# A recurrent-memory attention layer and its gradients: 32-row slots in four head groups, with the first eight rows of every segment batched outside the chains

## The chip, the cores and the metric

The kernel runs on one core of one Trainium2 chip. The metric is the device time of one execution in microseconds (us). A time below is the median of several executions, with the lowest and highest where they matter. A ratio is the mean time of one kernel's fast runs over the mean of the fast runs of the kernel before in the same rounds on the same chip, so it is not quite the ratio of the medians quoted beside it.

Names of the engines in the profile: PE is TensorE (matmul), PEld its weight load, DVE is VectorE, ACT is ScalarE, POOL is GpSimd, SP is SyncE; SPq, ACTq and POOLq are the queues from which these engines issue DMAs.

## The reference, cut to what matters

The reference computes a layer and all its gradients. The expensive half is attention with a recurrent memory: the sequence of 2,048 rows is cut into 64 segments of 32; in front of each stand 8 memory rows, which are the outputs of the 8 memory rows of the segment before.

```python
# B,S,Dm = 1,2048,512 ; H,Dh = 32,128 ; M,seg = 8,32 ; bf16
xn = layernorm(x); mem = mem0
mask = (idx[:,None] < M) | (idx[:,None] >= idx[None,:])      # memory rows see all 40
for s in range(64):
    h = concat([mem, xn[:, 32*s:32*s+32]])                    # 40 rows
    q, k, v = h@Wq, h@Wk, h@Wv                                # per head
    p = softmax(where(mask, q@k.T * Dh**-0.5, -1e9))
    o = einsum('hte,hed->td', p@v, Wo)
    mem = o[:8]; outs.append(o[8:])
out = x + concat(outs) + mlp(xn)         # mlp: relu(xn@w1+b1)**2 @ w2 + b2, F = 1792
# returned: out and the gradients of x, mem0, Wq, Wk, Wv, Wo, w1, b1, w2, b2
```

Forward and backward are therefore two chains of 64 dependent segments. One fact is used by the change: every row of a segment sees the memory rows, a segment row sees only earlier segment rows, and only the output of the 8 memory rows is carried on.

## The kernel before

Everything is laid out with the 40 rows of a segment on 40 of the 128 partitions. Projections go two at a time, one on rows 0 to 39 and one on rows 64 to 103 of the result; softmax works on 40 partitions x 12 heads; P is turned on PE, head by head.

```python
def proj2(dst, col0, nch):                 # two 512-column chunks at a time
    for fj in range(0, nch, 2):
        for dc in range(DC):
            nc.tensor.matmul(psA[:], lhsT=hT[:, dc, :], rhs=Wqkv[:, dc, ...], tile_position=(0, 0))
            nc.tensor.matmul(psB[64:64 + L, :], lhsT=hT[:, dc, :], rhs=Wqkv[:, dc, ...], tile_position=(0, 64))
        nc.any.tensor_copy(dst[...], psA[:]); nc.any.tensor_copy(dst[...], psB[64:64 + L, :])
# ... softmax on [40, 12 heads, 40] pieces, three pieces a segment ...
for i in range(nh):                        # P and gS are turned on PE, 40x40 at a time
    transpose_to(ps[:, i * L:(i + 1) * L], Pb[:, hh, :])
# ... the backward chain stores its gradients transposed, 960 KB a segment:
dma(S_GQKVT[s], gqkvT_s[:])
# ... and a stage after the chains loads them (segt), sums the input gradient in PSUM (ps_gxnA),
#     turns them and stores them in natural order (S_GN); then the weight gradients load S_GN.
```

Of the kernel before, what the change touches and what calls it, by code (L numbers as in the profile page):

```python
# [12 lines left out]
P = 128  # L13
# [13 lines left out]
def kernel(  # L27
# [71 lines left out]
    psp = ctx.enter_context(tc.tile_pool(name="psp", bufs=8, space=bass.MemoryType.PSUM))  # L99
    dram = ctx.enter_context(tc.tile_pool(name="dram", bufs=1, space=bass.MemoryType.DRAM))  # L100

    def pst(shape, dt=F32, name="ps"):
        return psp.tile(shape, dt, name=name, tag="ps")

    S_HN = dram.tile([NROWS, D], BF16, name="S_HN")
# [6 lines left out]
    S_ON = dram.tile([NROWS, HD], BF16, name="S_ON")  # L112
    S_GMEM = dram.tile([NSEG * M, D], BF16, name="S_GMEM")
    S_QKN = dram.tile([NSEG, L, 2 * HD], BF16, name="S_QKN")
    S_VT = dram.tile([NSEG, P, H, L], BF16, name="S_VT")
    S_P = dram.tile([NSEG, L, H, L], BF16, name="S_P")
    S_GQKVT = dram.tile([NSEG, P, 3, H, L], BF16, name="S_GQKVT")
    S_GN = dram.tile([NROWS, 3 * HD], BF16, name="S_GN")
# [8 lines left out]
    maskb = const.tile([L, L], F32, name="maskb")  # L127
    nc.gpsimd.memset(maskb[:], 0.0)
    nc.gpsimd.affine_select(
        maskb[:], maskb[:], pattern=[[-1, L]], compare_op=ALU.is_ge, fill=-1e9, base=0, channel_multiplier=1  # L130
    )
    nc.gpsimd.memset(maskb[0:M, :], 0.0)
    maskrep = const.tile([L, GMAX, L], F32, name="maskrep")
    for j in range(GMAX):
        nc.vector.tensor_copy(maskrep[:, j, :], maskb[:])
    ones_col = const.tile([P, 1], BF16, name="ones_col")
    nc.vector.memset(ones_col[:], 1.0)
    zeros_bf = const.tile([P, D], BF16, name="zeros_bf")
    nc.vector.memset(zeros_bf[:], 0.0)
    NCG = 4  # L140
    assert H % NCG == 0 and (3 * H) % NCG == 0 and M <= 32
    sel8 = const.tile([P, M], F32, name="sel8")
    nc.gpsimd.memset(sel8[:], 0.0)
    for g in range(NCG):
        nc.gpsimd.affine_select(
            sel8[:], sel8[:], pattern=[[-1, M]], compare_op=ALU.not_equal, fill=1.0, base=-32 * g, channel_multiplier=1
        )
# [7 lines left out]
    with tc.tile_pool(name="p0", bufs=1) as p0:  # L155
        xnN = p0.tile([P, TC, D], BF16, name="xnN")
        with tc.tile_pool(name="p0a", bufs=1) as p0a:
            xN = p0a.tile([P, TC, D], BF16, name="xN")
            dma(xN[:], xflat.rearrange("(c p) d -> p c d", p=P))
            ssum = p0a.tile([P, TC], F32, name="ssum")  # L160
            nc.vector.tensor_reduce(ssum[:], xN[:], axis=AX.X, op=ALU.add)
            nc.scalar.mul(mean_t[:], ssum[:], 1.0 / D)
            xc = p0a.tile([P, TC, D], BF16, name="xc")
            nc.vector.tensor_tensor(
                out=xc[:], in0=xN[:], in1=mean_t[:].unsqueeze(2).to_broadcast([P, TC, D]), op=ALU.subtract
            )
            sq = p0a.tile([P, TC, D], BF16, name="sq")
            nc.vector.tensor_tensor(out=sq[:], in0=xc[:], in1=xc[:], op=ALU.mult)
            var_t = p0a.tile([P, TC], F32, name="var_t")
            nc.vector.tensor_reduce(var_t[:], sq[:], axis=AX.X, op=ALU.add)  # L170
            veps = p0a.tile([P, TC], F32, name="veps")
            nc.vector.tensor_scalar(
                out=veps[:], in0=var_t[:], scalar1=1.0 / D, scalar2=EPS, op0=ALU.mult, op1=ALU.add
            )
            sdev = p0a.tile([P, TC], F32, name="sdev")
            nc.scalar.sqrt(sdev[:], veps[:])
            nc.vector.reciprocal(rstd_t[:], sdev[:])
            nc.vector.tensor_tensor(
                out=xnN[:], in0=xc[:], in1=rstd_t[:].unsqueeze(2).to_broadcast([P, TC, D]), op=ALU.mult
            )  # L180
        dma(S_HN[0:S, :].rearrange("(c p) d -> p c d", p=P), xnN[:])
        xnT = p0.tile([P, DC, S], BF16, name="xnT")
        gN = p0.tile([P, TC, D], BF16, name="gN")
        dma(gN[:], gflat.rearrange("(c p) d -> p c d", p=P))
        gT = p0.tile([P, DC, S], BF16, name="gT")
        npb = 1024 // P
        for src, dstT in ((xnN, xnT), (gN, gT)):
            for dc in range(DC):
                c0 = 0
                while c0 < TC:  # L190
                    n = min(npb, TC - c0)
                    ps = pst([P, n * P], BF16, name="ps_tr")
                    for j in range(n):
                        transpose_to(ps[:, j * P:(j + 1) * P], src[:, c0 + j, dc * P:(dc + 1) * P])
                    nc.any.tensor_copy(dstT[:, dc, c0 * P:(c0 + n) * P], ps[:])
                    c0 += n
        dma(S_XNT[:], xnT[:])
        dma(S_GT[:], gT[:])
        ps = pst([1, D], F32, name="ps_gb2")
        for c in range(TC):  # L200
            nc.tensor.matmul(ps[:], lhsT=ones_col[:, :], rhs=gN[:, c, :], start=(c == 0), stop=(c == TC - 1))
        gb2 = p0.tile([1, D], F32, name="gb2")
        nc.vector.tensor_copy(gb2[:], ps[:])
        gb2b = p0.tile([1, D], BF16, name="gb2b")
        nc.vector.tensor_copy(gb2b[:], gb2[:])
        dma(out_10.rearrange("(o n) -> o n", o=1), gb2b[:])

        with tc.tile_pool(name="p1", bufs=1) as p1, tc.tile_pool(name="p1b", bufs=2) as p1b:
            W1 = p1.tile([P, DC, F], BF16, name="W1")
            dma(W1[:], B_w1.rearrange("(c p) f -> p c f", p=P))  # L210
            W2 = p1.tile([P, FC, D], BF16, name="W2")
            dma(W2[:], B_w2.rearrange("(c p) d -> p c d", p=P))
            W1T = p1.tile([P, FC, D], BF16, name="W1T")
            for fc in range(FC):
                nc.sync.dma_start_transpose(W1T[:, fc, :], B_w1[:, fc * P:(fc + 1) * P])
            W2T = p1.tile([P, DC, F], BF16, name="W2T")
            for dc in range(DC):
                nc.sync.dma_start_transpose(W2T[:, dc, :], B_w2[:, dc * P:(dc + 1) * P])
            b1T = p1.tile([P, FC], F32, name="b1T")
            b1Tb = p1.tile([P, FC], BF16, name="b1Tb")  # L220
            dma(b1Tb[:], B_b1.rearrange("(c p) -> p c", p=P))
            nc.vector.tensor_copy(b1T[:], b1Tb[:])
            b2bc = p1.tile([P, D], BF16, name="b2bc")
            dma(b2bc[:], B_b2.rearrange("(o n) -> o n", o=1).partition_broadcast(P))
            gb1 = p1.tile([P, FC], F32, name="gb1")
            nc.vector.memset(gb1[:], 0.0)
            RCB = RB // P
            for rb in range(NRB):
                r0 = rb * RB
                rT = p1.tile([P, FC, RB], BF16, name="rT")  # L230
                aT = p1.tile([P, FC, RB], BF16, name="aT")
                gh1T = p1.tile([P, FC, RB], BF16, name="gh1T")
                for fc in range(FC):
                    ps = pst([P, RB], F32, name="ps_h1")
                    for dc in range(DC):
                        nc.tensor.matmul(
                            ps[:], lhsT=W1[:, dc, fc * P:(fc + 1) * P], rhs=xnT[:, dc, r0:r0 + RB],
                            start=(dc == 0), stop=(dc == DC - 1),
                        )
                    nc.scalar.activation(rT[:, fc, :], ps[:], ACT.Relu, bias=b1T[:, fc:fc + 1], scale=1.0)  # L240
                    nc.vector.tensor_tensor(out=aT[:, fc, :], in0=rT[:, fc, :], in1=rT[:, fc, :], op=ALU.mult)
                    ps2 = pst([P, RB], F32, name="ps_ga")
                    for dc in range(DC):
                        nc.tensor.matmul(
                            ps2[:], lhsT=W2T[:, dc, fc * P:(fc + 1) * P], rhs=gT[:, dc, r0:r0 + RB],
                            start=(dc == 0), stop=(dc == DC - 1),
                        )
                    nc.vector.scalar_tensor_tensor(
                        out=gh1T[:, fc, :], in0=ps2[:], scalar=2.0, in1=rT[:, fc, :], op0=ALU.mult, op1=ALU.mult
                    )  # L250
                    gtmp = p1b.tile([P, 1], F32, name="gtmp")
                    nc.vector.tensor_reduce(gtmp[:], gh1T[:, fc, :], axis=AX.X, op=ALU.add)
                    nc.vector.tensor_tensor(out=gb1[:, fc:fc + 1], in0=gb1[:, fc:fc + 1], in1=gtmp[:], op=ALU.add)
# [553 lines left out]
```

## Time and profile before

6585.92 us (three runs, 6579.46 to 6588.76). The first fence is the head of the profile page: the span, then the busy share in tenths of each of 40 slices (PEclk is the granted TensorE clock), then the chain of work that ended last, by engine and by line.

```profile
span 6580.5 us, 136014 instructions
PE   4965777777667676765677777777777778888998
DVE  5504555555555555554333333333333323331000
PEclk8997888888877888777666666666666679999999
DMA  4354111111111111112211211111111156666555
PE 61%; DVE 18%; ACT 9%; DMA 7%; issue 4%; SPq 1%; ACTq 0%; DVEq 0%
```

The second fence has the busy time in five stretches. Its columns are the stretch, its length, then busy us (and number of instructions) of PE, PEld, DVE, ACT and POOL, the granted clock, the DMA share and GB/s.

```profile
0.00:553.00 553.00, 364.95 (x2086) 177.66 (x2122) 191.77 (x339) 109.84 (x156) 1.76 (x14) 0.92 0.50 160
553.00:3090.00 2537.00, 1773.13 (x24241) 1112.19 (x24254) 1471.16 (x2712) 1207.26 (x1880) 0.00 (x0) 0.80 0.15 47
3137.00:5320.00 2183.00, 1555.80 (x27004) 1029.30 (x27003) 758.14 (x1536) 663.54 (x1086) 0.00 (x0) 0.65 0.19 63
5320.00:5955.00 635.00, 507.93 (x3808) 304.45 (x3840) 213.84 (x338) 278.17 (x222) 0.00 (x0) 0.90 0.68 225
5955.00:6580.00 625.00, 588.45 (x2887) 270.99 (x2944) 40.88 (x64) 68.72 (x112) 0.00 (x0) 0.99 0.55 161
```

The two chains take 2,537 and 2,183 of 6,580 us (72%). In them no engine is full: PE is busy for 70%, DVE for 58% and 35%, and the DMA engines for less than a fifth. Each is a line of dependent steps, one segment after the other, at about 40 and 34 us a segment. Only the last stage, the weight gradients, is dense (PE 94%, full clock).

Three groups show the kind of step. Columns: line, engine, operation, out<-in, shapes, count; busy us and mean ns of one; idle time just before them, and what ended most of it.

```profile
L395 PE MATMUL ps_pA<-Wqkv,hT 128*40 128x512 bf16 x3072 | 754.9, 406 | 22.4 <-DVE hT L387 11.6
L153 PE MATMUL ps_PT<-ident,Pb 40*40 40x40 bf16 x2048 | 102.8, 200 | 503.0 <-DVE Pb L451 503.0
L446 ACT ACTIVATE sm_t<-sm_t 40x480 f32<-40x480 f32 (+1 forms) x192 | 104.9, 558 | 400.9 <-DVE sm_t L442 400.9
```

PE idles for 503 us before the transposes of P and waits for the softmax there: the softmax itself runs on 40 of 128 lanes.

### The profile page before, as it was taken

The page shows a single profiled execution, that of the slowest core. Times are in us where ns is not written, and L with a number is a line of the kernel's source. Part 1 is how long each engine was busy: PE and PEld are TensorE (multiplying, and loading weights), DVE is VectorE, ACT ScalarE, POOL GpSimd, SP SyncE. Part 2 cuts the span into 40 slices and gives each one's busy share as a digit, 9 for nine tenths or more (in the row PEclk, how much of TensorE's full clock was granted, in tenths as well). Part 3 has the DMA queues.
Part 4 walks back from the last instruction along what each step waited for, and adds up shares of the span by engine and source line. Part 5 has one row for each costly group of instructions (what it writes and reads, how often), then busy time and mean ns, then how long its engine had stood idle before and what let it go on. Part 6 is the DMA issues. An engine that isn't in the chain of part 4 may idle for free.

```text
span 6580.5 us, 136014 instructions
## 1 busy us (share of the span) xinstructions
PE 4790.8 (73%) x60031; PEld 2895.1 (44%) x60170; DVE 2677.7 (41%) x4993; ACT 2328.8 (35%) x3457; POOL 1.8 (0%) x14
## 2 busy tenths in 40 slices
PE   4965777777667676765677777777777778888998
PEld 2423444444444444443444444444444445554443
DVE  5504555555555555554333333333333323331000
ACT  2303444444444444443223333233333244441110
POOL 0000000000000000000000000000000000000000
PEclk8997888888877888777666666666666679999999
DMA  4354111111111111112211211111111156666555
GB/s 146 113 171 158 51 53 53 54 51 52 52 38 39 38 43 42 41 40 112 87 64 65 66 66 58 64 65 64 66 63 60 61 177 225 228 200 189 162 163 152
DMA packets 294402, 607.73 MB, mean 92 GB/s; under 512 B 68641, under 2 KB 125618, under 8 KB 288946
## 3 DMA queue, kind: packets, MB, share of 16 engines
q1 hardware_dynamic: 293810, 599.03, 28.2%
q8 instruction: 470, 7.70, 0.5%
q14 instruction: 122, 1.00, 0.1%
HBM read 309.21 MB, written 286.01 MB: 90 GB/s over the span
## 4 chain that ended last, share of the span: by engine, by line
PE 61%; DVE 18%; ACT 9%; DMA 7%; issue 4%; SPq 1%; ACTq 0%; DVEq 0%
PE ps_pA L395 10%; PE ps_gw L744 5%; PE ps_gxnA L673 5%; PE ps_gOT L557 4%; ACT goNg L600 4%; PE ps_goN L153 4%; PE ps_omn L153 3%; DVE Rbf L489 2%; PE ps_A L504 2%; PE ps_gwo L766 2%; DVE sm_sum L448 2%; PE ps_qkT L153 2%; DMA S_GN<-gNpt 2%; DVE sb_t L574 2%; DVE sb_r L573 2%
## 5 line engine op out<-in xcount | busy, mean ns | idle before, releaser
L395 PE MATMUL ps_pA<-Wqkv,hT 128*40 128x512 bf16 x3072 | 754.9, 406 | 22.4 <-DVE hT L387 11.6
L400 PE MATMUL ps_pB<-Wqkv,hT 128*40 128x512 bf16 x3072 | 755.3, 406 | 2.9 <-DVE ONp L516 2.6
L395 PEld LDWEIGHTS <-hT 128*40 128x40 bf16 x3072 | 313.7, 106 | 378.1 <-issue 92.7
L153 PE MATMUL ps_PT<-ident,Pb 40*40 40x40 bf16 x2048 | 102.8, 200 | 503.0 <-DVE Pb L451 503.0
L407 DVE CAST qkN<-ps_pB 40x512 bf16<-40x512 f32 x481 | 331.3, 693 | 214.0 <-PE ps_pB L400 212.4
L673 PE MATMUL ps_gxnA<-WT,gblk 128*128 128x512 bf16 x1504 | 351.3, 394 | 45.6 <-ACT gblk L655 20.6
L405 ACT CAST qkN<-ps_pA 40x512 bf16<-40x512 f32 x480 | 274.9, 580 | 239.7 <-PE ps_pB L400 228.5
L153 PE MATMUL ps_gsT<-ident,gs 40*40 40x40 bf16 x2048 | 102.5, 199 | 318.4 <-DVE gs L578 318.3
L557 PE MATMUL ps_gOT<-goutT,WoT 128*128 128x40 bf16 x8192 | 270.0, 197 | 77.6 <-DMA b_vT<-S_VT 46.9
L400 PEld LDWEIGHTS <-hT 128*40 128x40 bf16 x3072 | 313.6, 106 | 22.9 <-issue 10.1
L623 PEld LDWEIGHTS <-gqkvT_s 128*8 128x8 bf16 x6144 | 175.4, 109 | 317.2 <-issue 249.5
L153 PEld LDWEIGHTS <-Pb 40*40 40x40 bf16 x2048 | 81.9, 113 | 523.2 <-DVE Pb L451 517.0
L600 ACT COPY goNg<-ps_goN 40x1024 bf16<-40x1024 bf16 x256 | 257.8, 1007 | 132.4 <-PE ps_goN L153 132.4
L557 PEld LDWEIGHTS <-WoT 128*128 128x128 bf16 x8192 | 263.5, 108 | 83.3 <-issue 47.0
L153 PE MATMUL ps_goN<-ident,gOT 128*40 128x128 bf16 x2048 | 266.2, 311 | 0.0
L673 PEld LDWEIGHTS <-gblk 128*128 128x128 bf16 x1536 | 154.7, 101 | 237.8 <-issue 35.7
L446 ACT ACTIVATE sm_t<-sm_t 40x480 f32<-40x480 f32 (+1 forms) x192 | 104.9, 558 | 400.9 <-DVE sm_t L442 400.9
L571 DVE TENSOR_TENSOR sb_t<-ps_gP,b_P 40x480 f32<-40x480 f32 (+1 forms) x192 | 108.2, 589 | 302.3 <-PE ps_gP L567 302.3
L153 PEld LDWEIGHTS <-gs 40*40 40x40 bf16 x2048 | 81.6, 113 | 338.7 <-DVE gs L578 332.5
L588 ACT COPY gsT<-ps_gsT 40x1000 bf16<-40x1000 bf16 x64 | 63.1, 986 | 437.2 <-PE ps_gsT L153 437.2
L153 PE MATMUL ps_omn<-ident,OT 128*8 128x128 bf16 x2048 | 214.3, 298 | 0.0
L407 DVE CAST vN<-ps_pB 40x512 bf16<-40x512 f32 x256 | 177.4, 693 | 82.4 <-PE ps_pB L400 82.4
(3795 smaller groups left out, 10595.5 us busy)
## 6 DMA issues: line engine op xcount, KB each, us to landing
S_GQKVT<-gqkvT_s SPq DMA_DIRECT2D x64, 960.0 KB
segt<-S_GQKVT SPq DMA_DIRECT2D x64, 960.0 KB
S_GN<-gNpt SPq DMA_DIRECT2D x192, 256.0 KB
S_QKN<-qkN SPq DMA_DIRECT2D x64, 640.0 KB
S_VT<-vT SPq DMA_DIRECT2D x64, 320.0 KB
b_vT<-S_VT SPq DMA_DIRECT2D x64, 320.0 KB
qNg<-S_QKN SPq DMA_DIRECT2D x256, 80.0 KB
kNg<-S_QKN SPq DMA_DIRECT2D x256, 80.0 KB
```

The costliest lines, as they stand in the source:

```text
L153: nc.tensor.transpose(ps_ap, in_ap, ident[base:base + k, base:base + k])
L395: nc.tensor.matmul(psA[:], lhsT=hT[:, dc, :], rhs=Wqkv[:, dc, col0 + fj * 512:col0 + (fj + 1) * 512], start=(dc == 0), stop=(dc == DC - 1) ...
L400: nc.tensor.matmul(psB[64:64 + L, :], lhsT=hT[:, dc, :], rhs=Wqkv[:, dc, col0 + (fj + 1) * 512:col0 + (fj + 2) * 512], start=(dc == 0), st ...
L405: nc.any.tensor_copy(dst[:, fj * 512:(fj + 1) * 512], psA[:])
L407: nc.any.tensor_copy(dst[:, (fj + 1) * 512:(fj + 2) * 512], psB[64:64 + L, :])
L448: nc.vector.tensor_reduce(sm[:, :nh], st[:, :nh, :], axis=AX.X, op=ALU.add)
L489: nc.any.tensor_copy(Rbf[32 * g:32 * g + M, :], Rs[g][32 * g:32 * g + M, :])
L557: nc.tensor.matmul(ps[:, i * L:(i + 1) * L], lhsT=WoT[:, dc, hh * P:(hh + 1) * P], rhs=goutT[:, dc, :], start=(dc == 0), stop=(dc == DC - 1),)
L600: nc.any.tensor_copy(goNg[:, :nh * P], psn[:])
L623: nc.tensor.matmul(Rs[g][32 * g:32 * g + M, :], lhsT=gqkvT_s[:, t, hh, 0:M], rhs=WT[:, t, hh, :], start=(k == 0), stop=(k == per - 1), til ...
L673: nc.tensor.matmul(psx[:], lhsT=gblk[:, t, hh, :], rhs=WT[:, t, hh, :], start=(cnt == 0), stop=(cnt == 3 * H - 1))
L744: nc.tensor.matmul(pss[i][:], lhsT=gn[:nr, i * P:(i + 1) * P], rhs=HNc[:nr, rc, :], start=(rc == 0), stop=(rc == RC_ALL - 1))
```

## The change

The intent is to fill the 128 partitions in the chains and to shorten them. Each segment becomes a slot of 32 rows: the 8 memory rows and the last 24 rows of the segment. The 32 heads form four groups of 8; group g uses rows 32g to 32g+31 of every tile, so four projections, score matmuls and so on run side by side. The first 8 rows of each segment are no input of the chain but keys of the slot: their projections (16 blocks, each with the 32 first rows of four segments) are computed before the forward chain, and their attention and its gradient in a stage between the chains ("left" in the kernel's names, "the remaining rows" below). The head groups leave four partial rows each, which GpSimd adds afterwards. The core of the diff (1,493 lines; "# ..." marks cuts):

```diff
-                            nc.tensor.matmul(
-                                psB[64:64 + L, :], lhsT=hT[:, dc, :],
-                                rhs=Wqkv[:, dc, col0 + (fj + 1) * 512:col0 + (fj + 2) * 512],
-                                start=(dc == 0), stop=(dc == DC - 1), tile_position=(0, 64),
# ...
+        def proj_half(dst, hT, W, col0, B):
+            ps = pbig("ps_proj")
+            for dc in range(DC):
+                for g in range(HG):
+                    c = col0 + g * GW + B * 512
+                    nc.tensor.matmul(ps[32 * g:32 * g + 32, :], lhsT=hT[:, dc, :], rhs=W[:, dc, c:c + 512],
+                                     start=(dc == 0), stop=(dc == DC - 1), tile_position=(0, 32 * g))
+            nc.any.tensor_copy(dst[:, B * 512:(B + 1) * 512], ps[:])
# ... P and gS are turned on DVE:
+                nc.vector.transpose(PT[:, :, i, :], Pb[:, B * KK:(B + 1) * KK, o:o + 32])
# ... gradients are turned in the chain and spilled in natural order:
+        def spill_nat(gX, t, r0):
+            gN = bs.tile([P, GW], BF16, name="gNat", tag="gNat")          # bs: 2 buffers
+            for B in range(2):
+                ps = trp.tile([P, 1024], BF16, name="ps_nat", tag="tr")
+                # ... four transposes on PE
+                nc.any.tensor_copy(gN[:, B * 512:(B + 1) * 512], ps[:, 0:512])
+            dma(S_G[r0:r0 + 32, t, :].rearrange("r (g c) -> g r c", g=HG), gN[:])
# ... sums of the four partial rows:
+    def sum_rows(pool, src_ra, src_rl, b):
+        for g in range(HG):
+            R1 = pool.tile([P, D], F32, name="R1", tag="R1")
+            dma(R1[:], src_ra[b, g].rearrange("j r d -> (j r) d"))
+            for j in range(SPB):
+                dma(R1[32 * j:32 * j + M, :], src_rl[b, g, M * j:M * j + M, :])
+            # ... nc.gpsimd.tensor_tensor(out=acc, in0=acc, in1=R1, op=ALU.add)
# ... stage of the remaining rows, per block b: loads, attention, its gradient, then
+            acc = sum_rows(lr, S_RA[0], S_RL[0], b)                       # lr: 3 buffers
+            memb = sum_mem(lr, S_RA[0], b)
# ... after the backward chain:
+        for b in range(NB - 1, -1, -1):
+            left_done(b)          # back-projection and spill of the block's remaining rows
+            finish_back(b)        # sums, layer-norm gradient; br: 2 buffers
```

## The prediction

> # Prediction
>
> **What bounds it now.** By the stretches of busy time and the chain of waits, five stages run in series: front and feed-forward part to 520 us; weight load 33; forward chain of 64 segments 553 to 3090 us, 39.9 each; backward chain 3137 to 5320, 34.1 each; then input gradient and spills (633) and weight gradients (625). The chains are 72% of the span and latency-bound: PE 70% busy, DVE 35 to 58%, DMA under 0.2. The timeline of a forward segment: projections and flips 14 us (a pair of matmuls each 0.215), softmax on 40 partitions 11, PV and transposes 5, memory sum 10. Backward: dP softmax 7, four copy-bound groups of 2.5, gR 8.2 (four matmuls per 0.43 while the clock is halved, then per 0.215), memory sum 4.
>
> **What changes.** Four head groups fill 128 partitions: softmax pieces shrink from 40x480 (0.59 us) to 128x160, estimated at 0.25; P and gS turn on DVE, not PE; projections go four at a time. The first eight rows' projections leave the chain.
>
> *Forward segment*: 24 projection slots 5.2 us, 32 transposes at 0.11 = 3.5, 96 small matmuls at gP's pace of 0.035 = 3.4, Wo 1.7, sum 1. The end is serial: softmax 2.4, PV 1.1, copy 0.65, transposes 0.45, copy 0.65, Wo 1.1, copy 0.65, sum 1, copy 0.25. With some cold clock and mode changes (the Trainium skill, "TensorEngine Tiling (Array Packing)", Key Properties, says a change of tiling mode drains the array; the trace shows no separate drain so far) 19.5 us; 64 make 1,250.
>
> *Backward segment*: projection, flip, dP 4.5, two DVE passes 3, outer products with 24 small evictions 3 exposed, gR 5.2 partly cold, sum 2: 19.5 us; 1,250.
>
> **What it adds.** (1) 64 DMA transposes of 256 KB between the feed-forward part and its weight gradients, two buffers per kind; ghn loads stand behind them in the one SP queue. Before's W2T transposes issue at 2.0 us each; with landings about 3 us per transpose: PE idle 190 us, front 700. (2) First rows' projection 16 x 8 = 125. (3) Left stage, 16 blocks of 27 us (PE 20, ACT 19): 430. (4) The tail: 16 back-projections, and sums of four partial rows on POOL. The skill ("GPSIMD Engine Reference", 3.1, Elementwise) has 4.5 us for an fp32 add of 2048, so I estimate 1.2 for 512; the trace before has no POOL add. One free buffer makes load, add, load serial: 37 us a block, 600, mostly behind the weight-gradient matmuls (1,920 x 0.215 = 413), then 640 x 0.215 = 138 of gWo that need the last sum: 790, for 1,258 before.
>
> **Sum.** 733 front and load + 125 + 1,250 + 430 + 25 + 1,250 + 790 = about 4,600 us; range 4,100 to 5,150. Faster by over 2%: 0.97; within 2%: 0.02; slower: 0.01.
>
> **What would show it.** In the timeline: segment pitch 17 to 23 us in both chains; a PE gap near 320 us of 120 to 250 filled with DMA transposes; left stage 20 to 35 us a block; after the backward chain, POOL adds of R1 paced by their loads, and gWo waiting for GOc. PE instructions fall from 120,000 to 103,000.
>
> **What would make it wrong.** Small tiled matmuls slower than 0.035 us or mode changes of 0.2 us each (segments of 25 us or more); the clock halved in the chains; DMA transposes at 100 GB/s or less (front up by 100 us more); the in-order SP queue stalling loads behind stores in chains and tail.

## The result, and the profile after

The changed kernel is correct and takes 5742.35 us (four runs, 5716.52 to 5747.22) beside 6587.31 us for the kernel before (6579.46 to 6588.76): ratio 0.871, 95% interval 0.869 to 0.873. It is 13% faster. It is also about 1,140 us slower than predicted, and above the range.

The head of the profile page, as before:

```profile
span 5745.4 us, 121908 instructions
PE   3923588888888884555376666767667644899009
PEclk8966898888888886565577777777777777899559
DMA  5296553333333325455543433333333334666222
PE 49%; DMA 25%; DVE 11%; ACT 7%; SPq 4%; issue 3%; POOL 2%; DVEq 0%; POOLq 0%; ACTq 0%
PE ps_gR L677 9%; DMA S_G<-gNat 9%; PE ps_proj L423 7%; PE ps_gw L929 7%; PE ps_tr L201 6%; PE ps_R L524 4%; PE ps_out L666 3%; PE ps_gwo L942 2%; PE ps_m L620 2%; PE ps_wgh L474 1%; DMA gXL<-S_GL 1%; ACT OT L433 1%; DMA S_PART<-part 1%; PE ps_bm L894 1%; DMA S_WT<-wtt 1%
```

The chain that ended last was 61% PE and 7% DMA. It is now 49% PE and 25% DMA, and one transfer, the store of gNat to S_G, stands second in the list by line with 9%. The stretches, with the columns of before:

```profile
0.00:712.00 712.00, 357.19 (x1970) 171.30 (x1970) 183.47 (x317) 102.40 (x143) 8.71 (x44) 0.81 0.60 171
712.00:863.00 151.00, 123.18 (x1789) 51.53 (x1790) 41.48 (x60) 57.93 (x99) 6.02 (x20) 0.90 0.58 212
863.00:2176.00 1313.00, 1087.48 (x17024) 525.92 (x17024) 406.71 (x1156) 526.93 (x1022) 66.44 (x186) 0.83 0.33 106
2176.00:2862.00 686.00, 321.98 (x6082) 197.52 (x6083) 214.79 (x624) 224.98 (x707) 155.70 (x148) 0.59 0.53 170
2862.00:4555.00 1693.00, 1166.31 (x20948) 664.24 (x20948) 455.94 (x2046) 502.50 (x1276) 16.31 (x61) 0.75 0.38 111
4555.00:5745.00 1190.00, 714.00 (x4483) 321.93 (x4481) 66.51 (x145) 110.75 (x194) 187.54 (x160) 0.79 0.44 144
```

| stage | before | predicted | after | missed by |
|---|---|---|---|---|
| front, feed-forward part, weight load | 553 | 733 | 712 | -21 |
| first rows' projection | in the chain | 125 | 151 | +26 |
| forward chain | 2,537 (about 40 a segment) | 1,250 (19.5) | 1,313 (20.7) | +63 |
| remaining rows (16 blocks) and hand-over | in the chain | 430 + 25 (27 a block) | 686 (38.4 a block) | +231 |
| backward chain (with 47 us before it) | 2,230 (34.1 a segment) | 1,250 (19.5) | 1,693 (26.6) | +443 |
| tail: input gradient, weight gradients | 1,260 | 790 | 1,190 | +400 |
| sum | 6,580 | about 4,600 | 5,745 | +1,142 |

The forward chain did what was hoped. Three stages missed, and these are the subject of the experiments. (Here and below the length of a segment is the time from the first to the last start of its Wqkv or gv-gradient matmuls, divided by 63; that of a block of the remaining rows the time from the first to the last start of the transposes of its q, divided by 15.)

The groups that carry the waits, with the columns of before:

```profile
L201 PE MATMUL ps_tr<-ident,gON 128*128 128x128 bf16 x640 | 88.6, 287 | 327.8 <-DVE gNat L691 322.5
L942 PE MATMUL ps_gwo<-GOc,on_71965 128*128 128x512 bf16 x160 | 36.5, 392 | 273.4 <-DMA GOc<-S_GO 273.4
```

PE idles for 328 us before the transposes of gON, and what ends this is a copy of gNat, which belongs to the segment before. The timeline of a backward segment shows how (columns: start in us, length, engine, line, operation, count; in brackets the idle time before and its releaser):

```profile
3519.13 1.60 SPq L692 DMA_DIRECT2D S_G<-gNat  x2
...
3520.19 0.61 PE L201 MATMUL ps_nat<-ident,gq 128*128 128x128 bf16 x8
...
3526.98 0.58 ACT L691 COPY gNat<-ps_nat 128x512 bf16<-128x512 bf16 x1 [5.23 <-DMA S_G<-gNat]
3527.01 0.42 DVE L691 COPY gNat<-ps_nat 128x512 bf16<-128x512 bf16 x1 [6.85 <-DMA S_G<-gNat]
...
3527.48 0.59 PE L201 MATMUL ps_tr<-ident,gON 128*128 128x128 bf16 x4 [5.29 <-DVE gNat L691]
```

A segment spills three gradients (gv, gk, gq) through gNat, which has two buffers. The two stores are issued from 3519.13 on. The third spill's transposes run at 3520.19, but its copies must wait until a buffer is free, which is at 3526.98, about 7.8 us after the store was issued. Until then the two PSUM buffers shared by all transposes are full, so PE cannot turn the next segment's gON; it starts nothing else meanwhile and idles for 5.3 us. The same wait stands 63 times in the view of the waits of this chain (columns: engine, line, releaser: us in total, times, longest):

```profile
DVE gNat L691 <- DMA S_G<-gNat: 420.8, 63, 6.9
PE ps_tr L201 <- DVE gNat L691: 322.5, 63, 5.4
```

In the tail PE stops for 273 us before the last weight gradient and waits for GOc, that is for the last row sum.

### The profile page after: what moved, and what is told of

The parts are those of the page before. It is cut to its first block, busy times and chain, and to the rows that moved or that the text cites. A ratio compares the mean times of both kernels' runs of the same rounds, so it can differ in the third digit from the quotient of the medians.

```text
span 5745.4 us, 121908 instructions
## 1 busy us (share of the span) xinstructions
PE 3770.1 (66%) x52292; PEld 1932.4 (34%) x52292; DVE 1368.9 (24%) x4348; ACT 1525.5 (27%) x3440; POOL 440.7 (8%) x619
## 4 chain that ended last, share of the span: by engine, by line
PE 49%; DMA 25%; DVE 11%; ACT 7%; SPq 4%; issue 3%; POOL 2%; DVEq 0%; POOLq 0%; ACTq 0%
PE ps_gR L677 9%; DMA S_G<-gNat 9%; PE ps_proj L423 7%; PE ps_gw L929 7%; PE ps_tr L201 6%; PE ps_R L524 4%; PE ps_out L666 3%; PE ps_gwo L942 2%; PE ps_m L620 2%; PE ps_wgh L474 1%; DMA gXL<-S_GL 1%; ACT OT L433 1%; DMA S_PART<-part 1%; PE ps_bm L894 1%; DMA S_WT<-wtt 1%
## 5 line engine op out<-in xcount | busy, mean ns | idle before, releaser
L423 PE MATMUL ps_proj<-Wqkv,hT 128*32 128x512 bf16 x6144 | 488.1, 423 | 0.3 <-DVE hT L572 0.3
L929 PEld LDWEIGHTS <-HNc 128*128 128x128 bf16 x1920 | 188.2, 98 | 265.2 <-issue 40.0
L691 ACT COPY gNat<-ps_nat 128x512 bf16<-128x512 bf16 x241 | 141.1, 585 | 496.4 <-DMA S_G<-gNat 431.8
L524 PE MATMUL ps_R<-Wo,OT 128*32 128x512 bf16 x2048 | 172.5, 469 | 86.2 <-ACT OT L433 86.2
L677 PE MATMUL ps_gR<-WT_28394,gv 128*32 128x512 bf16 x2048 | 224.0, 615 | 0.0
L423 PEld LDWEIGHTS <-hT 128*32 128x32 bf16 x6144 | 151.5, 102 | 172.9 <-issue 72.7
L423 PE MATMUL ps_proj<-WoT,goT 128*32 128x512 bf16 x2048 | 159.8, 386 | 39.2 <-POOL goT L841 39.2
L677 PE MATMUL ps_gR<-WT_28396,gk 128*32 128x512 bf16 x2048 | 166.5, 483 | 0.0
L666 PE MATMUL ps_out<-gST,b_kN 32*128 32x32 bf16 x2048 | 129.6, 184 | 30.0 <-DVE gkL L877 23.6
L666 PE MATMUL ps_out<-gST,b_kLs 8*128 8x32 bf16 x2048 | 124.6, 183 | 0.8
```

The costliest lines, as they stand in the source:

```text
L423: nc.tensor.matmul(ps[32 * g:32 * g + 32, :], lhsT=hT[:, dc, :], rhs=W[:, dc, c:c + 512], start=(dc == 0), stop=(dc == DC - 1), tile_posit ...
L524: nc.tensor.matmul(R[32 * g:32 * g + 32, :], lhsT=OT[:, k, g, :], rhs=Wo[:, g * KH + k, :], start=(k == 0), stop=(k == KH - 1), tile_posit ...
L666: nc.tensor.matmul(p3[:, k, :], lhsT=N_[32 * g:32 * g + m, k * P:(k + 1) * P], rhs=X(k)[32 * g:32 * g + m], start=(i == 0), stop=(i == len ...
L677: nc.tensor.matmul(R[32 * g:32 * g + 32, :], lhsT=gX[:, k, g], rhs=WT[t][:, g * KH + k, :], start=(i == 0), stop=(i == 3 * KH - 1), tile_p ...
L691: nc.any.tensor_copy(gN[:, B * 512:(B + 1) * 512], ps[:, 0:512])
L929: nc.tensor.matmul(ps[:], lhsT=HNc[:, rc, dc * P:(dc + 1) * P], rhs=gn[:, rc, u * 512:(u + 1) * 512], start=(rc == 0), stop=(rc == RC_ALL ...
```

## The experiments

Eighteen kernels were run, all correct, each timed in three rounds. The expectations, written before the runs, name theories by letters. A: the backward chain waits for the spill store, because gNat has two buffers; A1: that store is slow because of its shape. C: the tail is long because its work sits alone on one in-order queue and on POOL. E and F: the stage of the remaining rows lacks buffers, or is bound by dependent work at a low clock. G: it is held by the one in-order queue which it shares with the row sums. H and J: what is put into the backward chain costs time because its spill stores (H) or its loads (J) stand behind other transfers in that queue. The rivals stand in the expectations.

The table has what each run measured; the stages are read from its profile. The last column is the time from the last gradient projection of gv to the end.

| run | us | ratio | backward segment | block of remaining rows | after the last gv gradient |
|---|---|---|---|---|---|
| changed kernel | 5742 | 0.871 | 26.6 | 38.4 | 1,196 |
| e1_spill6 | 5414 | 0.821 | 21.4 | 38.5 | 1,197 |
| e2_spill_split | 5465 | 0.831 | 23.7 | 38.3 | 1,111 |
| e3_r1_6 | 5659 | 0.860 | 26.6 | 38.4 | 1,116 |
| e4_left2 | 5703 | 0.866 | 26.6 | 36.8 | 1,193 |
| e5_hoist | 5211 | 0.792 | 27.5 | 38.4 | 613 |
| e6_fsums | 5751 | 0.875 | 29.6 | 28.4 | 1,192 |
| e7_wtr | 5630 | 0.856 | 26.6 | 38.4 | 1,195 |
| e8_all | 5291 | 0.805 | 33.1 | 28.5 | 606 |
| e9_nofs | 5197 | 0.790 | 28.6 | 38.4 | 630 |
| e10_spill6_split | 5311 | 0.808 | 21.4 | 38.2 | 1,102 |
| e11_pref | 5203 | 0.791 | 28.7 | 38.3 | 629 |
| e12_spread | 5330 | 0.810 | 33.2 | 28.5 | 640 |
| e13_actload | 4961 | 0.754 | 25.0 | 38.4 | 634 |
| e14_actload_all | 5121 | 0.778 | 29.7 | 28.6 | 626 |
| e15_leftq | 5713 | 0.867 | 26.6 | 37.5 | 1,197 |
| e16_leftpool | 5728 | 0.872 | 26.6 | 32.9 | 1,195 |
| e17_poolq | 4951 | 0.754 | 25.1 | 33.3 | 631 |
| e18_poolboth | 4940 | 0.752 | 25.0 | 33.2 | 606 |

### The backward chain: the spill store

**e1_spill6** gives gNat six buffers instead of two.

```diff
-            gN = bs.tile([P, GW], BF16, name="gNat", tag="gNat")
+            gN = bs.tile([P, GW], BF16, name="gNat", tag="gNat", bufs=6)
```

> Changed kernel, with six buffers instead of two for the spill tile gNat. Theory A (the backward chain's extra 7 us a segment is PE, in order, stuck behind the third spill, whose buffer waits 7.8 us for a store to land): the 5.3 us stall per segment goes, the clock is halved for less of the segment, pitch from 26.4 to 20 to 21.5 us, total 5,350 to 5,450 us. Rival B (the pitch is the real length of the dependent work, small matmuls and mode changes, and the stall merely fills a wait): pitch stays above 25, total above 5,650.

Measured: 5414.31 us (5371.82 to 5421.56), 328 us less. The segment fell from 26.6 to 21.4 us. In the waits of the same chain no wait for S_G is left among the longest; the first lines are these (the first is POOL, which has nothing else to do):

```profile
POOL goT L899 <- PE ps_proj L423: 1292.1, 61, 26.6
DVE gNat L691 <- PE ps_nat L201: 768.6, 189, 11.2
```

A fixed stretch of both chains shows that the clock came back with it. First the changed kernel, then e1_spill6; PE does 24% more work in the same 1,300 us, at a granted clock of 0.80 instead of 0.75.

```profile
2900.00:4200.00 1300.00, 894.62 (x16064) 509.57 (x16057) 349.69 (x1568) 385.58 (x979) 13.10 (x49) 0.75 0.38 112
```

```profile
2900.00:4200.00 1300.00, 1108.72 (x19968) 610.18 (x19964) 455.76 (x1952) 473.90 (x1220) 16.03 (x60) 0.80 0.43 138
```

So the missing 5 us a segment are the wait for the spill store, and not the arithmetic or slower small matmuls.

**e2_spill_split** keeps two buffers and issues each spill as four stores, one for each head group.

```diff
-            dma(S_G[r0:r0 + 32, t, :].rearrange("r (g c) -> g r c", g=HG), gN[:])
+            for g in range(HG):
+                dma(S_G[r0:r0 + 32, t, g * GW:(g + 1) * GW], gN[32 * g:32 * g + 32, :])
```

> Changed kernel, two spill buffers, but each spill store issued as four stores of 32 rows (one per head group) with the same bytes and addresses. Theory A1 (the store is slow because a transfer whose outermost dimension is 4 runs on 4 of the 16 DMA engines): landing falls from 7.8 us to 3 to 4 us, the stall falls to under 1.5 us, pitch 21 to 23, total 5,400 to 5,520. Rival A2 (the store waits in general traffic or behind the queue): landing and stall unchanged or worse because four issues cost more of the queue, total 5,700 or more.

Measured: 5465.28 us (5437.26 to 5488.02). The segment is 23.7 us, and in the timeline PE's stall is half of what it was (2.6 us, it was 5.3); both are above what was expected (23 and 1.5). Of the 277 us gained, 85 lie in the tail, which spills through the same function. Over the whole run the copies of gNat waited 198 us for the store, where they had waited 960:

```profile
3500.72 0.58 ACT L691 COPY gNat<-ps_nat 128x512 bf16<-128x512 bf16 x1 [0.69 <-DMA S_G<-gNat]
3501.36 0.61 PE L201 MATMUL ps_tr<-ident,gON 128*128 128x128 bf16 x8 [2.56 <-ACT gNat L691]
```

A page has a reason why the store was slow. The Trainium skill, "DMA: Bandwidth & Descriptors", section "Why a DMA increments its semaphore by 16 and not by 1", says that a transfer is spread over the largest number of DMA engines, at most 16, which divides the slowest dimension larger than 1 of both its patterns. The spill's pattern is 4 x 32 x 1024, so it would use 4 of 16 engines; with 32 rows outermost it would use 16. The kept traces agree with the page, for they hold the semaphore updates by which each transfer reports its landing. In the backward chain every one of 190 stores of the changed kernel shows one update at 0.9 us and four later ones, the last 7.6 us after the issue (median; 5.7 to 10.3). Every one of the 760 quarter stores of e2_spill_split shows sixteen, the last after 2.6 us; all four quarters of a spill had landed 4.2 us after the first issue (expected: 3 to 4). These counts fit 4 engines and 16, and theory A1.

**e10_spill6_split** does both.

> The changed kernel with six gNat buffers and with the spill stores split by head group. If after six buffers no wait for the spill store is left in the backward segment (21.4 us there), the split adds nothing and the total is within 1% of the 5414 us of six buffers alone, or a little slower because of four times the store issues on the queue. If a wait was left, the segment falls to about 19.5 us, the predicted length, and the total to about 5300 us.

Measured: 5310.72 us (5309.42 to 5317.75). The segment is 21.4 us, exactly that of six buffers, so in the chain no wait was left that the split could take away. The total was expected within 1% of 5414 and is 1.9% lower, mostly because the tail, which spills through the same function, became 95 us shorter.

What remains between the predicted 19.5 us and 21.4 us was not taken apart by a run; the trace shows two candidates. A DVE piece of 128x160, estimated at 0.25 us, takes 0.31 to 0.33 in the timeline; and the gR matmuls (they give the gradient of the slot's input rows) are 35% of the chain that ended last in a window of e10_spill6_split's backward stage. There all 1,504 of those for gv ran at the halved clock (mean 629 ns) and all of those for gq at the full one (379 ns).

### The tail: one queue, and work put behind work

**e3_r1_6** gives the tile R1, through which the tail's row sums go, six buffers instead of two.

```diff
-            R1 = pool.tile([P, D], F32, name="R1", tag="R1")
+            R1 = pool.tile([P, D], F32, name="R1", tag="R1", bufs=RB1.get(id(pool)))
# ... with RB1[id(br)] = 6, and 6 for gb4 and prod4
```

> Changed kernel, with six buffers instead of two for the R1 tiles of the last backward sums. Theory C (the tail is load, add, load through one free buffer, 46 to 63 us a block, and gWo waits 273 us for it): 25 to 35 us a block, wait of gWo under 80 us, total 5,450 to 5,560. Rival D (the tail is paced by the in-order queue and the small loads themselves): 40 us or more a block, total above 5,650.

Measured: 5658.69 us (5654.9 to 5659.17), 84 us less. PE no longer waits for GOc: a block's sums took 32.6 us, where they had taken 63.3 (from the first to the last start of the addition that makes gx, 4587.2 to 5076.1 and 4625.3 to 5574.2, divided by 15). But the weight gradients now start at 5099 instead of 4912: the sums and the loads of the weight gradients stand in one queue that is served in order, and with more buffers the compiler's scheduler, which decides the order on each queue, placed all sums first: all 380 loads of these sums were issued before the first load of gn, where in the changed kernel 114 of 382 were. The wait was turned into another one. These are the instructions of the weight gradients in e3_r1_6, first of the tile ps_gw and then of GOc (min/median/max ns, first and last start):

```profile
L932 PE MATMUL ps_gw<-gn,HNc x1920: 379/379/631, 5099.4 to 5515.2; 128*128 128x512 bf16 x192
```

```profile
L945 PE MATMUL ps_gwo<-GOc,on x640: 379/379/380, 5515.4 to 5653.3; 128*128 128x512 bf16 x160
```

**e5_hoist** takes the tail's work apart: `left_done` and `finish_back` of a block are issued inside the backward chain, one block behind; gNat and R1 have three buffers.

```diff
+            if j == 2 and b + 1 < NB:
+                left_done(b + 1)
+            if j == 1 and b + 1 < NB:
+                finish_back(b + 1)
-        for b in range(NB - 1, -1, -1):
-            left_done(b)
-            finish_back(b)
+        left_done(0)
+        finish_back(0)
```

> The back-projection of each block's remaining segment rows and the sums of its gradient are taken out of the tail and issued inside the backward chain, one block behind; three gNat buffers and three R1 buffers. If the tail of 1190 us is long because this work sits alone on one in-order DMA queue and on the row-sum engine (theory C), it shrinks to the weight gradients alone, about 413 + 138 us and some 50 us of fill, so 600 to 650 us; the backward segment stays near 24 us (it was 26.5 with two gNat buffers and 21.4 with six), since it gains only about 8 us of TensorE work in four segments, and the whole falls to 5000 to 5150 us. Rival: the chain has no room for it, because its DMA queue or the row-sum engine is already full there; then the segment grows by 6 us or more and the whole stays over 5350 us.

Measured: 5210.57 us (5204.09 to 5215.1). The tail fell from 1,196 to 613 us, as expected: 416 us of gWq, gWk, gWv, 138 of gWo, 60 of start-up. The chain was not free: its segment is 27.5 us, 6 us more than with six spill buffers alone, where 2 to 3 us were expected. So of 583 us taken from the tail, about 380 came back in the chain, if e1_spill6 is taken as the measure of what it could have been. Not all of this need be the hoisted work: with three gNat buffers PE still waited 143 us in the chain for copies of gNat (2.3 us a segment), and no run hoisted the work with six.

**e7_wtr** concerns the one gap that was predicted well: 64 transposing weight loads during which PE idles in the front. It moves them into the forward loop, one each segment.

```diff
-            with tc.tile_pool(name="wtr", bufs=2) as wtr:
-                # ... 64 dma_start_transpose and stores
+            if jobs:
+                turn_weights(*jobs.pop(0))        # in the forward loop
```

> The 64 transposing weight loads, during which TensorE idled for 173 us in the front of the changed kernel, are issued one per segment inside the forward chain. If the chain has DMA and queue room for them, the front ends near 525 us instead of 699 and the whole gains 150 to 175 us, the forward segment staying at 20.5 us. Rival: a transposing load holds the queue for about 2.7 us and delays the chain's own stores, so the forward segment grows by 2 us or more and the gain is under 50 us.

Measured: 5629.91 us (5613.65 to 5634.35), 112 us less; the forward segment did not change (20.6 us). But the mechanism was another: the trace has the transposes of Wq, Wk and Wv between 348 and 581 us, that is, still in the front; those of Wo follow until 706 us, before the forward chain starts. So the run did not test whether the chain has room for them. The scheduler, free to place them, put them beside the feed-forward part's weight gradients instead of ahead of them.

### The loads of the chain behind the sums

**e9_nofs** joins e5_hoist, e7_wtr and the split spill; **e8_all** adds e6_fsums (below).

> The same as the run with all repairs, but the forward row sums stay in the stage of the remaining rows. Expected 4950 to 5050 us if theory H is right (100 to 150 us slower than with all), and equal to or faster than it under the rival.

> All repairs together: tail work inside the backward chain (three gNat and three R1 buffers), spill stores split by head group, forward row sums inside the backward chain, transposing loads inside the forward chain. If the repairs add, the sum from the measured ones is 5211 (hoisted tail) minus 112 (transposes) minus 150 (remaining rows' stage, whose block fell to 28.4 us) minus 60 to 150 (split spill stores in the chain), so 4800 to 4900 us. Theory H (my reading of the run that moved the forward sums alone: the gain was given back because the chain's spill stores stand behind the added loads in the queue, with two gNat buffers) says that with spill stores that land sooner most of the 150 us is kept. Rival: the chain's queue is full, and moving the forward sums into it gives the 150 us back again; then this run is not faster than the same kernel without that move.

Measured: e9_nofs 5197.25 us, e8_all 5291.35. Both missed by far: the front became 100 us shorter, yet e9_nofs is only 13 us faster than e5_hoist, since its segment grew to 28.6 us. The rival of theory H was right: what is put into this chain comes back. The waits of e9_nofs name it: ten times in 1,200 us, which is about once in every block of four segments, PE waits some 23 us for the loaded v.

```profile
PE ps_sc L430 <- DMA b_vT<-S_VTA: 231.3, 10, 24.1
```

**e11_pref** issues the six loads of a segment one segment earlier in the program, ahead of the hoisted work.

```diff
+            if s > 0:
+                nxt = load_seg(s - 1)          # b_part, b_qN, b_kN, b_kLs, b_vT, b_P
             if j == 2 and b + 1 < NB:
                 left_done(b + 1)
```

> The kernel of e9_nofs with one change: the six loads of a backward segment are issued before the hoisted sums and back-projection of the segment ahead of it, not after them. Theory J: in e9_nofs, once per block, the chain waited some 23 us for its loaded v (10 waits, 231 us in a window of 1200 us), because those loads stand in the one in-order queue behind row-sum loads that wait for the row-sum engine. Then these waits go and the backward segment falls from 28.6 us to 23 or 24 us, the whole from 5197 to about 4880 us (4820 to 4950). Rival: the queue itself is full (bandwidth of issue), or the chain stands behind the row sums on the row-sum engine itself, which also copies the next segment's rows; then the wait only changes its name and the whole stays over 5100 us.

Measured: 5203.31 us, no change, and the wait is still there (235 us). This did not refute theory J, it failed to test it. The queue's own timeline shows the order in which the scheduler left it: b_part goes at 3506, but the next loads, b_qN and so on, only after the sums and after the store of their result, at 3529.6.

```profile
3506.00 0.35 SPq L849 DMA_DIRECT2D b_part<-S_PART  x1
...
3526.42 1.28 SPq L842 DMA_DIRECT2D S_GO<-memb  x4
3527.79 1.71 SPq L698 DMA_DIRECT2D S_G<-gNat  x4
3529.60 0.56 SPq L851 DMA_DIRECT2D b_qN<-S_QA  x1
```

**e12_spread** adds the forward sums and cuts all sums into four parts, one for each segment of a block.

> e11_pref and, with it, the forward row sums in the backward chain, with all sums cut into four parts, one in each segment of a block. Under theory J the 150 us of the remaining rows' stage are now kept: 4700 to 4850 us, segment at most 25 us. Under the rival the segment grows to 29 us or more, and the run is slower than e11_pref.

Measured: 5329.86 us, segment 33.2 us. Slower than e11_pref, like e8_all; PE's wait for the loaded v is still there (333 us in 1,200, 17 times).

**e13_actload** changes the queue and not the order: the six loads of e11_pref are issued from ScalarE.

```diff
-            dma(vT[:], S_VTA[s])                     # dma = nc.sync.dma_start
+            nc.scalar.dma_start(vT[:], S_VTA[s])     # and so for all six
```

> The kernel of e11_pref, with the six loads of a backward segment issued from ScalarE's own queue instead of the shared one. Theory J: the waits for the loaded v (235 us in a window of 1200 us) go, the segment falls from 28.6 to 23 or 24 us and the whole from 5203 to about 4880 us (4800 to 4950). Rival: the row sums or the DMA engines hold the chain whatever queue the loads use; then the segment stays over 27 us and the whole over 5100 us. A cost of theory J's test: six issues of some 0.4 us, 2.5 us a segment, on ScalarE, which is busy for 29% of that stage.

Measured: 4961.38 us (4956.16 to 4972.89), 242 us less than e11_pref. The wait for b_vT is gone from the list, the segment is 25.0 us (expected 23 or 24), and PE did this in the same 1,200 us (first e11_pref, then e13_actload):

```profile
3000.00:4200.00 1200.00, 816.74 (x14689) 449.45 (x14678) 332.34 (x1383) 349.00 (x882) 129.80 (x142) 0.77 0.48 134
```

```profile
3000.00:4200.00 1200.00, 944.40 (x16958) 520.14 (x16947) 436.94 (x1708) 359.70 (x898) 153.02 (x167) 0.80 0.57 157
```

So theory J holds for this wait: the loads stood in an in-order queue behind transfers that waited for the row sums. The Trainium skill, "DMA: Bandwidth & Descriptors", section "Issuing engines are not separate DMA queues", says that transfers of all issuing engines run on the same 16 DMA engines, and that using several "will only save the time on the sequencer it takes to initiate the DMA, which is usually small relative to the DMA itself". Here the six issues take about 0.33 to 0.54 us each, but the gain was 3.7 us a segment: what counted was not the time to issue but the waiting of what stood ahead.

**e14_actload_all** is e12_spread with the loads on ScalarE's queue.

> The kernel of e12_spread (forward row sums in the backward chain too, sums spread over the four segments of a block) with the loads on ScalarE's queue. Theory J: the stage of the remaining rows keeps its 28 us a block and the segment is 23 to 25 us: the whole 4700 to 4830 us. Rival: segment over 28 us as in e12_spread, whole over 5200 us.

Measured: 5121.03 us, segment 29.7 us. 209 us better than e12_spread, so the loads' queue mattered here too, but 160 us worse than e13_actload: the forward sums cost more in the backward chain than they save in their own stage, whatever queue the loads use. By the waits of this run POOL waits 528 us in 1,200 for loads of partial rows and 280 for the others; its sums are not done in time, and the hoisted back-projection, which shares the queue with them, makes PE wait (95 us for gXL).

### The stage of the remaining rows

**e4_left2** gives this stage's tiles two buffers instead of one and the sums six instead of three.

```diff
-    with sb("ls", 1) as ls, sb("ld", 2) as ld, sb("lsm", 2) as lsm, sb("lr", 3) as lr, \
+    with sb("ls", 2) as ls, sb("ld", 2) as ld, sb("lsm", 2) as lsm, sb("lr", 6) as lr, \
# ... two weight loads are moved behind the stage to make room
```

> Changed kernel, with two buffers for every tile of the left stage and six for its row sums; to make room WT1 and WT2 are loaded at the start of the backward chain, which may cost 10 to 20 us there once. Theory E (the left stage's 38 us a block instead of 27 are waits for single buffers: part for its store, loads of l_kM and l_vM): 25 to 29 us a block, total 5,560 to 5,620. Rival F (the block is its dependent work at half clock, so buffers don't matter): 35 us or more a block, total 5,720 or more.

Measured: 5702.55 us (5677.95 to 5706.06), 36.8 us a block where 25 to 29 were expected. Missing buffers are at most a small part of the loss.

**e6_fsums** moves only the forward row sums, their output and the memory sums from this stage into the backward chain.

```diff
-            acc = sum_rows(lr, S_RA[0], S_RL[0], b)      # and what follows, in the stage
+            if j == 3:                                   # in the backward chain
+                finish_fwd(b)
```

> Only the forward row sums, their output and the memory sums move from the stage of the remaining rows into the backward chain. Theory G: that stage's 38.4 us a block are the shared in-order DMA queue and the row sums in it, so the block falls to 25 to 29 us and the stage gains 130 to 200 us; some 40 to 60 us of that may come back in the backward chain. Theory F: its block is bound by the dependent attention work at the low granted clock (0.60), and stays at 35 us or more; then the whole is within 60 us of the changed kernel's 5742 us.

Measured: 5751.05 us: no gain in total, but 28.4 us a block. Without the sums the attention work of a block takes about what the prediction said (27 us), though the granted clock from 2230 to 2690 us was low in both kernels (0.59 in the changed kernel, 0.63 here); this rules theory F out. The transposes of q, one group of eight for each block, show it (first the changed kernel, then e6_fsums; min/median/max ns, first and last start):

```profile
L201 PE MATMUL ps_tr<-ident,l_qN x128: 219/314/315, 2213.9 to 2789.9; 128*128 128x128 bf16 x128
```

```profile
L201 PE MATMUL ps_tr<-ident,l_qN x128: 219/314/314, 2207.0 to 2632.6; 128*128 128x128 bf16 x128
```

From the first projection of the forward chain to the first gradient of the backward chain it took 175 us less, and the backward chain gave it all back (29.6 us a segment, 3 more than before, times 63).

That the sums hold the block left two readings: their place in the shared queue (theory G), or the sums themselves.

**e15_leftq** issues the stage's loads from ScalarE; **e16_leftpool** issues all transfers of the sums from GpSimd's own queue, which leaves SyncE's queue to the attention work.

```diff
# e15_leftq, and so for l_kN, l_vN, l_kM, l_vM, l_gT
-            dma(qN[:], S_QL[b])
+            nc.scalar.dma_start(qN[:], S_QL[b])
# e16_leftpool
-            acc = sum_rows(lr, S_RA[0], S_RL[0], b)
+            acc = sum_rows(lr, S_RA[0], S_RL[0], b, nc.gpsimd.dma_start)
# ... and its other loads and stores
```

> The changed kernel with one edit: the six loads of a block of the remaining rows' stage are issued from ScalarE's queue; the row sums stay where they are. Theory G (shared in-order queue): the loads no longer stand behind the row sums, the block falls from 38.4 to 28 to 31 us and the whole to 5570 to 5640 us. Rival: it was the row sums' own work (their adds and transfers) that the move of e6_fsums took away, not the order in the queue; then the block stays at 35 us or more and the whole within 60 us of 5742.

> The changed kernel with one edit: all transfers of the forward row sums are issued from the row-sum engine's own queue, so that what waits for a sum waits there. Theory G (the shared in-order queue: loads and stores of the block stand behind transfers that wait for sums): the block falls from 38.4 us to 28 to 31 us, the whole to 5570 to 5640 us. Rival: the sums' own work (their transfers in the DMA engines, their adds, or now their issue in software) holds the block; then it stays at 35 us or more and the whole over 5680 us.

Measured: e15_leftq 5712.57 us, 37.5 us a block: the loads' place in the queue was not it. PE waited in another place (91 us in 300 for copies into part, whose stores still stood in the queue of the sums). e16_leftpool 5727.65 us: the blocks now follow each other at 32.9 us, but the whole did not change (ratio 0.872, before 0.871). The waits of the hand-over show where it went:

```profile
PE ps_proj L423 <- POOL goT L841: 116.0, 1, 116.0
```

The attention work ran ahead of the sums, and then PE waited 116 us until POOL had caught up, because POOL also prepares the first rows of the backward chain. The sums never became faster. Their output tile ob was made every 38.3 us in the changed kernel (first start 2267.8, last 2842.1), every 36.3 in e15_leftq and every 38.1 in e16_leftpool (first and last start at the end):

```profile
L770 POOL TENSOR_TENSOR ob<-R,bb x16: 1150/1152/1220, 2267.1 to 2811.8; 128x512 bf16<-128x512 f32 x16
```

```profile
L770 POOL TENSOR_TENSOR ob<-R,bb x16: 1144/1152/1218, 2256.6 to 2828.6; 128x512 bf16<-128x512 f32 x16
```

So theory G is wrong as stated. The row sums are a line of their own, with load, patch, add and memory sum one after the other, and they take 36 to 39 us a block on any queue that was tried; the stage goes at their pace. Of the 38 us POOL computes about 9 (six adds of 1.26, one of 1.15 and a copy of 0.6); the rest is waiting for loads, and in e16_leftpool issuing them at 0.5 to 0.6 us each. Which part of this waiting could be shortened most was not tried.

### The best version

**e17_poolq** is e13_actload with e16_leftpool's edit. **e18_poolboth** issues the backward sums from GpSimd as well.

> e13_actload with the edit of e16_leftpool. If theory G holds there, 4961 less 100 to 150: 4810 to 4860 us. If not, within 60 us of 4961.

> As e17_poolq, and the transfers of the backward row sums in the chain from the row-sum engine's queue too, so that the spill stores no longer stand behind them: the segment falls from 25 us towards 23 us, the whole to 4700 to 4800 us. Rival: some 45 issues a block in software make the row-sum engine the limit, and since it also copies each next segment's rows, the chain waits for it: segment over 27 us, whole over 4950 us.

Measured: 4951.16 us (4947.23 to 4958.67) and 4940.14 us (4932.76 to 4946.19). Neither gave what theory G promised; after e16_leftpool this is no surprise. e17_poolq has the ratio of e13_actload (0.754). e18_poolboth has a ratio of 0.752 (0.751 to 0.753) to the kernel before and the lowest median, about 800 us below the changed kernel; but these three lie within 0.5% of each other, and their 95% intervals overlap.

## Why the prediction was right or wrong

**Right.** The direction. The front: 712 us for 733, with PE idle while the transposes ran (8 us busy between 320 and 505). The forward chain: 20.7 us a segment for 19.5. Here only the sum was confirmed: its terms were not tested one by one, and at least two were off in opposite directions (the DVE pieces slower than estimated, the small matmuls faster), so part of the fit may be luck. PE and PEld instructions fell from 120,201 to 104,584 (predicted: 120,000 to 103,000). The POOL add of 128x512, estimated at 1.2 us from the 4.5 us that the Trainium skill, "GPSIMD Engine Reference", 3.1, gives for 2048 elements, took 1.26. Small matmuls were faster than the 0.035 us assumed: 32 in 0.90 us, or 0.028 each (the line below). No separate drain shows where the tiling mode changes: tiled matmuls of ps_sc start at 2866.34, just before the modelled end of untiled transposes at 2866.42.

```profile
2866.57 0.90 PE L666 MATMUL ps_out<-b_P,gON 32*128 32x40 bf16 x32
```

**Wrong: "Backward segment: ... 19.5 us; 1,250."** (+443 us). The sum listed the steps on PE, DVE and ACT and left out the spill: three gradients through two buffers, each free only when a store of 256 KB has landed, some 7.6 us later. The wait is exposed because the transposes of the spill share their two PSUM buffers with those of the next segment, and PE started nothing past them. e1_spill6 showed it: 5.2 us a segment, 328 us. The other 1.9 us a segment, about 120 us, stay open. The prediction had named "the in-order SP queue stalling loads behind stores in chains and tail" as a danger; here it was not the queue but the buffer's release.

**Wrong: the tail, "37 us a block, 600, mostly behind the weight-gradient matmuls"** (+400 us). The term was mis-sized: 63.3 us a block instead of 37, so 1,000 us of sums instead of 600. The starts of gx show two paces: 66 to 81 us a block until the weight gradients ended, and 46 to 55 in the last five intervals. So load, add, load was longer than 37 us even alone, and longer still beside other transfers. And less of them lay behind other work: the 16 back-projections came first with PE busy for 157 of 325 us, then the weight gradients ran dense for 412 us, then 273 us of sums were exposed before gWo. e3_r1_6 showed that with six buffers the sums take 32.6 us a block, but then delay the weight gradients, and e5_hoist that the work fits elsewhere: tail 613 us.

**Wrong: "Left stage, 16 blocks of 27 us (PE 20, ACT 19)"** (+231 us with the hand-over). The 27 us for the attention work were right (28.4 in e6_fsums). But the stage also has sums of four partial rows, the same kind of work to which the prediction gave 37 us a block in the tail, and in this stage it gave them nothing beyond the 27. A stage takes its slowest line, here 38 us of sums.

**Small misses.** First rows' projection 9.4 us a block for 8 (+26), forward chain +63.

**Open.** Why the hoisted chain of e13_actload still takes 25.0 us a segment and not 21.4 plus 2 of added PE work; how fast the sums could be made, for instance with fewer and larger loads; and whether the split spill, which issues four times as many stores, pays in e13_actload at all. All three were left untried.

## What to carry to other kernels

When a dense chain gets shorter, cost its spills like its arithmetic: for every tile that a store must release, compare the landing time with the time until the buffer is needed again, and give it more buffers before anything else; then look at the store's outermost dimension (here 32 rows instead of 4 groups cut the landing of a spill from 7.6 to 4.2 us). Before work is moved "behind" other work, ask which in-order queue both share and what its head waits for; a load that gates the chain should not stand in a queue behind transfers that wait for a slow engine. And work that is costed in one stage must be costed in every stage in which it appears.

## What the Trainium skill lacked or had wrong

- "DMA: Bandwidth & Descriptors", "Issuing engines are not separate DMA queues": it counts only the time to issue as the gain of a second issuing engine. In e13_actload the move of six loads a segment to ScalarE's queue took 242 us (5%) off, because they no longer waited behind transfers that wait for another engine. The page has the order within a queue but not this cost.
- The same page, on how many engines a transfer uses: the rule agreed with the traces of the changed kernel and of e2_spill_split, but the page gives no landing time for such a store. Here the 256 KB store with an outermost dimension of 4 landed 7.6 us after its issue (median of 190), and a quarter store of 32 rows after 2.6 us.
- No page that was read tells what a line of load, patch and add on GpSimd costs: 36 to 39 us a block for the forward sums in all versions that kept them in their stage, with about 9 us of computing. "GPSIMD Engine Reference", 3.1, agrees as to the add itself (4.5 us for 2048 elements, a quarter of which is 1.12; 1.26 us measured for 512).
- "TensorEngine Tiling (Array Packing)", Key Properties, says that a change of tiling mode drains the array, with no figure. In this case's traces no separate drain shows: at most changes of mode in the backward chain the next matmul starts about 0.07 us before the modelled end of the one before.
